# A fused linear attention and smoothed-ReLU MLP kernel: third group loaded whole, one table less, last output block in halves, a new order of the steps

## The chip, the cores and the metric

The kernel runs on one core of a Trainium2 chip. Its engines are TensorE (PE, with its weight loads listed apart as PEld), VectorE (DVE), ScalarE (ACT), GpSimd (POOL) and SyncE (SP), which issues most of the transfers. The metric is the time of one execution on the device in microseconds.

## The reference

Four sequences of 768 steps, 8 heads of 48 channels, go through a decayed linear attention; its output, seen as 3072 tokens of 384 channels, goes through an MLP with 2048 hidden channels.

```python
for t in range(S):                                   # r, k, v: (4, 8, 768, 48)
    cur = einsum('bhd,bhe->bhde', u * k[t], v[t])
    y[t] = einsum('bhd,bhde->bhe', r[t], state + cur)
    state = w[:, None] * state + einsum('bhd,bhe->bhde', k[t], v[t])
h = y.reshape(3072, 384) @ w_in                      # 384 x 2048
g = where(h >= 1, h, where(h <= -1, 0, (h + 1) ** 2 / 4))
out = g @ w_out                                      # 2048 x 384
```

## The kernel before

**Tiling.** Time is cut into 6 chunks of 128 steps. A unit is one sequence in one chunk; two units make a group, so there are 12 groups (0 to 11) and 24 units (0 to 23). Unit n is half n % 2 of group n // 2. Groups 0 and 1 are the first chunk. Within a chunk the recurrence becomes matrix products: A is K times R transposed, masked to AT; Y is AT times V plus R times the carried state; Sp is what the chunk adds to the state.

**The order.** The kernel is one list of words, ORDER, written out by hand (lines 24 to 59). The loop at its end (line 529) calls one function for each word, in that order, and every engine runs its own instructions strictly in the order in which they were issued. A word has the step's name, the group or unit, after a dot the half (or, for m, r, s, g, the quarter of the hidden channels, and for M first the half and then the quarter), after = the engine (V is DVE, A is ACT, G is POOL) and after / the PSUM banks. So the order of the words with one engine is that engine's queue, and a step waits behind all words of its engine that stand ahead of it.

**The steps.**
- LR, LK, LV: loads of r, k, v (line 252, on SP's queue); without a half, both halves in one transfer.
- ln, bw, bu, wq, wE, wC, uS, WupS, WdnS, Wup, Wdn: tables of powers of w and of u. Wup and Wdn write a second copy of a table to PSUM, which the scaled R and K of group 0 then read.
- Rs, Ks: R and K scaled by their tables. KU, RKU, us, B: the term of u.
- TR, TK, T: transposes on PE, copied out by cR, cK, c; from group 4 on RT and KT do it by a transposing transfer. A (and AA for both units), AT (mask, on DVE), V (cast of v, on ACT), Y, y and yg, X with its copy xc, from group 3 on xcg in place of both (a transposing transfer).
- Sp, Tm, decayg, sbf: the state.
- m: a quarter of the first projection, 12 matmuls of 256 columns into a pair of PSUM banks; r, s, g: its activation, on ACT, ACT and DVE. The pair is free when g is done.
- M: an eighth of the second projection, 4 matmuls of 384 columns; og or o copies the result out, stg or st stores it. WI and WO load w_in and w_out on POOL's queue, in 3 and 2 parts.
- Zs and Z: n matmuls on a tile of zeros, to keep PE running.

**PSUM.** Two pairs of banks (0 and 1) exist all the time. Four single banks serve groups 0 and 1; when the first step asks for pair 2 or 3, they are closed and become those two pairs (line 185).

**Around the change.** Group 2 is loaded in six halves (LR2.0 to LV2.1). Rs of group 0 reads the PSUM table of Wup. Group 11 has no group behind it: its two halves have a PSUM pair each and use only the first bank of the two, so each is copied (o11.0 on ACT, o11.1 on DVE) and stored on its own.

Of the kernel before, what the change touches and what calls it, by code (L numbers as in the profile page):

```python
# [73 lines left out]
def kernel(  # L74
# [35 lines left out]
    def copy(e, out, in_):  # L110
        nc.scalar.copy(out, in_) if e == "A" else engines[e].tensor_copy(out, in_)  # L111
# [379 lines left out]
    def do_M(e, b, g, jq):  # L491
        j, q = jq
        last = g == S // C * BP - 1
        key, k = (("op", g, j), 0) if last else (("op", g), j)
        if key not in tiles:
            tiles[key] = pair(b[0], F32, "op")
        wi, wo = part(q, OUT_PARTS)
        for f in range(FG):
            nc.tensor.matmul(  # L499
                tiles[key][:, k, :DO], tiles["g", g, q][:, f, j * P : (j + 1) * P], w_out_sb[wi][:, wo, f * DO : (f + 1) * DO],  # L500
                start=(q == 0 and f == 0), stop=(q == nQ - 1 and f == FG - 1),
            )
# [21 lines left out]
    def do_Z(e, b, n):  # L524
        for i in range(n):
            nc.tensor.matmul(tiles["z"][:, 0, :P], idle[:, :P], idle[:, :P], start=True, stop=True)

# [39 lines left out]
```

## Time and profile before

| | us |
|---|---|
| median of 3 runs | 174.38 |
| lowest and highest of them | 174.08, 174.93 |
| the profiled execution | 173.8 |
| span of its trace | 172.0 |
| PE busy in the span | 163.7 |
| DVE, ACT, POOL busy | 130.6, 130.0, 117.1 |

The span runs from the first instruction to the last; some 1.8 us of the execution lie around it. PE is busy for 95% of the span, the others for 68 to 76%. The granted TensorE clock is 1.00 in all of it. In rows of the trace a time is followed by the duration; a row with x60 stands for 60 instructions, and what stands in brackets is the idle time just before it and what ended it.

### The profile page before, as it was taken

How to read it: one execution, taken by the hardware profiler on the slowest of the kernel's cores; microseconds unless marked ns; L12 is line 12 of the kernel's file. 1: busy time of each engine (PE TensorE's matmuls, PEld its weight loads, DVE VectorE, ACT ScalarE, POOL GpSimd, SP SyncE). 2: the span in 40 equal slices, each digit the busy share in tenths (PEclk: the TensorE clock that was granted, in tenths of full speed). 3: DMA queues.
4: the chain of work that ended last, by engine and by line, in shares of the span. 5: the costliest groups of instructions: out<-in, count | busy, mean ns of one | idle time of the engine just before them, and what ended most of it. 6: DMA issues, size and time to landing. Idle time of an engine off the chain costs nothing.

```text
span 172.0 us, 4014 instructions
## 1 busy us (share of the span) xinstructions
PE 163.7 (95%) x1658; PEld 130.9 (76%) x1658; DVE 130.6 (76%) x149; ACT 130.0 (76%) x150; POOL 117.1 (68%) x85
## 2 busy tenths in 40 slices
...
GB/s 106 198 187 191 199 203 197 221 195 203 174 190 88 213 188 175 188 204 150 200 312 197 185 215 174 219 173 168 308 195 219 4 60 138 43 98 0 8 91 91
DMA packets 103591, 28.26 MB, mean 164 GB/s; under 512 B 98834, under 2 KB 102676, under 8 KB 103572
## 3 DMA queue, kind: packets, MB, share of 16 engines
...
q0 software_dynamic: 1744, 3.15, 10.0%
q8 instruction: 13, 0.21, 0.5%
...
q10 hardware_dynamic: 4, 0.00, 0.0%
...
## 4 chain that ended last, share of the span: by engine, by line
PE 81%; DMA 5%; SPq 4%; ACT 3%; POOL 2%; DVE 2%; issue 1%; DVEq 0%; POOLq 0%
PE hp L464 36%; PE op L499 34%; SPq L252 4%; PE A L359 3%; DMA Vi<-in_v_dram 3%; DMA xT<-y 2%; PE Y L427 2%; PE Y L421 2%; PE Sp L394 2%; ACT pt L475 1%; ACT Vb L111 1%; POOL V L302 1%; PE T L319 1%; DVE g L487 1%; POOL RKU L271 1%
## 5 line engine op out<-in xcount | busy, mean ns | idle before, releaser
L464 PE MATMUL hp<-xT,w_in 128*128 128x256 bf16 x576 | 69.1, 273 | 0.9 <-DMA xT<-y 0.5
L499 PE MATMUL op<-w_out,g 128*128 128x384 bf16 x384 | 68.4, 326 | 0.0
L487 DVE SCALAR_TENSOR_TENSOR g<-sq,hp 128x1024 bf16<-128x1024 bf16 x48 | 57.9, 1215 | 13.2 <-ACT sq L484 13.2
L464 PEld LDWEIGHTS <-w_in 128*128 128x128 bf16 x576 | 61.9, 114 | 4.2 <-issue 1.2
L475 ACT ACTIVATE pt<-hp 128x1024 f32<-128x1024 f32 x46 | 46.9, 1020 | 14.0 <-PE hp L464 14.0
L499 PEld LDWEIGHTS <-g 128*128 128x128 bf16 x384 | 36.3, 98 | 21.3
L484 ACT ACTIVATE sq<-pt 128x1024 bf16<-128x1024 f32 x46 | 48.3, 1057 | 1.2
L368 DVE TENSOR_TENSOR AT<-A,umask 128x1024 bf16<-128x1024 f32 x20 | 23.7, 1219 | 5.2 <-PE A L359 5.2
L271 POOL TENSOR_TENSOR Ks<-Ki,Wdn 128x768 bf16<-128x768 f32 (+1 forms) x12 | 20.2, 1684 | 7.4 <-DMA Ki<-in_k_dram 3.7
L302 POOL TENSOR_TENSOR V<-Vb,diag 128x768 f32<-128x768 bf16 (+1 forms) x14 | 18.1, 1292 | 10.2 <-DVE diag L293 4.4
L271 POOL TENSOR_TENSOR RKU<-Ri,KU 128x768 f32<-128x768 f32 (+1 forms) x13 | 21.2, 1631 | 1.2 <-DVE KU L271 0.8
L405 POOL TENSOR_TENSOR state<-Tm,wCm 128x768 f32<-128x768 f32 x8 | 14.6, 1822 | 10.6 <-DVE Tm L402 10.6
L271 POOL TENSOR_TENSOR KU<-Ki,u_sb 128x768 f32<-128x768 f32 (+1 forms) x13 | 21.2, 1632 | 0.4 <-DMA Ki<-in_k_dram 0.3
L271 POOL TENSOR_TENSOR Rs<-Ri,Wup 128x768 bf16<-128x768 f32 x10 | 18.2, 1824 | 0.0
L439 DVE TENSOR_TENSOR y<-Y,V 128x768 bf16<-128x768 f32 x10 | 9.6, 956 | 5.9 <-PE Y L427 3.3
L111 ACT CAST Vb<-Vi 128x768 bf16<-128x768 f32 (+1 forms) x14 | 10.2, 734 | 4.8 <-DMA Vi<-in_v_dram 4.8
L293 DVE TENSOR_REDUCE diag<-RKU 128x16 f32<-128x768 f32 (+1 forms) x14 | 11.6, 830 | 1.5 <-POOL RKU L271 1.5
L111 ACT COPY o<-op 128x768 f32<-128x768 f32 (+1 forms) x9 | 6.9, 764 | 6.4 <-PE op L499 6.3
L111 ACT CAST state_bf<-state 128x768 bf16<-128x768 f32 (+1 forms) x12 | 8.5, 717 | 3.7 <-POOL state L405 3.7
L427 PE MATMUL Y<-Vb,AT 128*128 128x48 bf16 x192 | 10.2, 185 | 0.4 <-ACT Vb L111 0.4
L427 PEld LDWEIGHTS <-AT 128*128 128x128 bf16 x192 | 9.3, 97 | 0.7 <-issue 0.5
L402 DVE TENSOR_TENSOR Tm<-Sp,state 128x768 f32<-128x768 f32 x8 | 7.6, 956 | 2.7 <-PE Sp L394 2.7
...
## 6 DMA issues: line engine op xcount, KB each, us to landing
out_dram<-o SPq DMA_DIRECT2D x11, 384.0 KB, 3.9
Ki<-in_k_dram SPq DMA_DIRECT2D x9, 384.0 KB, 6.0
Ri<-in_r_dram SPq DMA_DIRECT2D x9, 384.0 KB, 6.1
Vi<-in_v_dram SPq DMA_DIRECT2D x9, 384.0 KB, 5.0
...
Ki<-in_k_dram SPq DMA_DIRECT2D x6, 192.0 KB, 3.9
Ri<-in_r_dram SPq DMA_DIRECT2D x6, 192.0 KB, 4.6
Vi<-in_v_dram SPq DMA_DIRECT2D x6, 192.0 KB, 5.4
```

What stands on the lines that cost most here:

```text
L111: nc.scalar.copy(out, in_) if e == "A" else engines[e].tensor_copy(out, in_)
L271: engines[e].tensor_mul(part(out)[:, :, :, :D], part(a), rep(b, j1 - j0) if len(b.shape) == 3 and b.shape[1] == H else part(b))
L293: nc.vector.tensor_reduce(d[:, hs], tiles["RKU", g][:, hs, :], AX.X, ALU.add)
L302: engines[e].tensor_mul(t[:, hs, :], tiles["V", g][:, hs, :], tiles["diag", g][:, hs].unsqueeze(2).to_broadcast([P, n, D]))
L368: nc.vector.tensor_mul(t.rearrange("p i n t -> p (i n) t"), tiles["A", n].rearrange("p i (n t) -> p (i n) t", t=P), umask.unsqueeze(1).to_ ...
L405: engines[e].tensor_mul(states[g % BP], tiles["Tm", g], flat(wCm).unsqueeze(1).to_broadcast([P, UNITS, DM]))
L427: nc.tensor.matmul(Y[:, h * D : (h + 1) * D], AT[:, i, p, :], V[:, j * H + h, :], start=(c == 0), stop=True, skip_group_check=True,)
L464: nc.tensor.matmul(hp[:, f, :], w_in_sb[wi][:, i, wo * FG * P + f : (wo + 1) * FG * P : FG], tiles["xT", g][:, :, i, :], start=(i == 0), s ...
L475: nc.scalar.activation(t, tiles["hp", g, q], AF.Relu, bias=0.5, scale=0.5)
L484: nc.scalar.activation(t, p, AF.Square)
L487: nc.vector.scalar_tensor_tensor(out=make("g", ("g", g, q), [P, FG, TOK], BF16), in0=tiles["sq", g, q], scalar=1.0, in1=tiles["hp", g, q], ...
L499: nc.tensor.matmul(tiles[key][:, k, :DO], tiles["g", g, q][:, f, j * P : (j + 1) * P], w_out_sb[wi][:, wo, f * DO : (f + 1) * DO], start=( ...
```

## The change

The list ORDER is replaced as a whole; the number of instructions of each kind stays, but for what follows.
- LR2, LK2, LV2 load group 2 in three transfers, where six were.
- The word Wup is gone, so Rs of group 0 reads the table in SBUF.
- Group 11 writes its second projection with 8 matmuls of 192 columns for each M, the two halves of the output columns in the two banks of the pair. M11.13 becomes MA11.13 and MB11.13, one for each half of the columns, and o11.1 and st11.1 become oA11.1, stA11.1, oB11.1, stB11.1.
- Some steps change engine. To DVE come KU0.1, Ks1.0, KU1.0, RKU1.0, cR0, cR1, cK2, cK3, wC, xc1, KU3, og0, c6, xc4, r2.2, og3 and og9; from DVE go uS, cR3, r1.2, c4, xc5, og4, og10 (to ACT), Rs1.0, Rs1.1 and RKU0.1 (to POOL); s0.2 goes from ACT to POOL.
- The PSUM banks of many steps change. The Z's are 19, 3, 10, 12, 9, 5 and 2 matmuls, 60 as before.
- The tile of zeros has 128 columns instead of 512. New functions gate, do_HR, do_HK and do_Zq are called by no word.

```diff
-Zs/0 ln Z19 bw/1 LK0.0 bu/0 uS=V LK1.0 LR0.0 LK0.1 LR0.1 LV0.0 wq/2 WdnS Ks1.0=G LR1.0 LR1.1 Wdn/3 Ks0.0=V Ks0.1=V
-TK0/0 Wup/1 Rs0.0=V TR0/3 LK1.1 cK0=A WupS KU0.1=G KU0.0=V RKU0.0=G cR0=A KU1.0=G LV0.1 Rs0.1=V Z2 TR1/1 A0/03 LV1.0
-LV1.1 WI0 WI1 WI2 us0.0 cR1=A TK1/1 cK1=A AT0.1 Z4 A1/13 Rs1.0=V LR2.0 LR2.1 Rs1.1=V V0.1 AT1.0 V0.0 Z9 TR3/1 B0.0=G
-AT1.1 RKU0.1=V wE AT0.0 wC=A us0.1 Z7 Y1/3 TR2/0 B0.1=G Y0/2 y0 y1 cR2=A RKU1.0=G Z8 X0/2 Z4 TK2/3 X1/0 Ks1.1=G xc0=A
-Sp1/2 cK2=A xc1=A Z7 TK3/3 cK3=A Tm1 A2/20 m0.0/0 cR3=V us1.0 AT2.1 AT2.0 r0.0=A A3/31 AT3.1 KU1.1=G RKU1.1=G m0.1/1
-V1.0 s0.0=A B1.0=G Sp2/2 AT3.0 us1.1 r0.1=A Tm2 Y2/3 y2 g0.0 V1.1 X2/0 LK2.0 Y3/1 B1.1=G s0.1=A LK2.1 Sp0/2 Sp3/3
-xc2=V LK3 y3 WO0 m0.3/0 r0.3=A s0.3=A g0.1 X3/1 Tm0 xc3=V m0.2/1 LR3 LV2.0 Tm3 m1.1/2 g0.3 r1.1=V m1.0/3 m1.2/0 Ks2=G
-r0.2=A s0.2=A g0.2 sbf2=A s1.1=A r1.0=A s1.0=A sbf3=A g1.1 m1.3/1 r1.2=V WO1 KU2=G LV2.1 M0.00/2 M0.10 M0.11 M0.01
-g1.0 M1.00/3 M1.10 M1.11 M1.01 Rs2=G s1.2=A g1.2 T5/0 RKU2=G LK4 r1.3=A s1.3=A g1.3 T4/1 LV3 Ks3=G M0.02 M0.03 LR4 us2
-c5=V A5/0 KU3=G Rs3=G c4=V A4/1 AT5 sbf1=A M1.02 M0.12 M0.13 AT4 T6/0 sbf0=A V2 Y4/1 Y5 B2=G og0=A T7/2 c6=A RKU3=G
...
-r3.2 s3.2=A KT5 m3.3/1 M3.00/3 M3.10 V5 B4=G AT8 Y8/2 Y9 r3.3 g3.2 s3.3=A LK8 M3.11 M3.12 M3.01 M3.02 yg4 AA5/20 g3.3
-M3.13 M3.03 xcg4 m4.0/1 LR7 KU5=G RKU5=G AT10 LK7 decayg3=G sbfg3=A Rs6=G og3=A us5 LV7 B5=G KU6=G RKU6=G r4.0 Sp8/2
...
-yg11 xcg11 m10.3/0 M10.00/3 g10.1 M10.10 r10.3 m10.2/1 s10.3=A g10.3 r10.2 M10.11 M10.01 s10.2=A m11.0/2 g10.2 r11.0
-m11.1/0 M10.02 M10.03 r11.1 s11.0=A m11.2/1 g11.0 M10.12 M10.13 s11.1=A r11.2 g11.1 m11.3/2 og10=V s11.2=A M11.10/0
-M11.11 g11.2 stg10 r11.3 s11.3=A M11.00/3 M11.01 M11.12 M11.02 g11.3 M11.13 M11.03 o11.1=V st11.1 o11.0=A st11.0
+Zs/0 LR0.0 LK0.0 LR0.1 LV0.0 LR1.0 ln Z19 bw/3 LK1.0 bu/1 WupS Rs0.0=V Rs0.1=V Wdn/0 LK0.1 WdnS uS=A KU0.0=V LV0.1
+TR0/2 RKU0.0=G wq/3 Ks0.0=V Rs1.0=G TK0/1 LR1.1 cR0=V wE wC=V LK1.1 WI0 us0.0 V0.0 TR1/2 KU0.1=V RKU0.1=G cK0=A Z3
+A0/31 Ks0.1=V Z10 TK1/0 cK1=A cR1=V LV1.0 AT0.0 LV1.1 WI1 V0.1 AT0.1 us0.1 Z12 A1/31 AT1.1 Sp0/2 Y0/0 B0.0=G AT1.0
+Rs1.1=G Z9 TR3/1 B0.1=G y0 Ks1.0=V Y1/3 y1 LR2 KU1.0=V WI2 cR3=A Z5 X0/1 xc0=A Z2 X1/0 xc1=V RKU1.0=V TR2/1 cR2=A Tm0
+TK2/3 cK2=V Ks1.1=G KU1.1=G m0.0/1 A2/10 us1.0 TK3/2 cK3=V AT2.0 AT2.1 m0.1/0 r0.0=A A3/23 s0.0=A r0.1=A AT3.0 Sp1/1
+Tm1 g0.0 RKU1.1=G V1.0 B1.0=G Sp2/0 Y2/2 AT3.1 m0.2/1 WO0 s0.1=A LK2 g0.1 us1.1 V1.1 B1.1=G Y3/1 LR3 y2 m0.3/0 r0.2=A
+Tm2 y3 r0.3=A s0.3=A X2/3 xc2=V Sp3/0 s0.2=G Tm3 X3/2 xc3=V m1.2/2 m1.0/3 LK3 g0.3 m1.1/0 Rs2=G WO1 r1.2=A s1.2=A g0.2
+g1.2 m1.3/1 r1.0=A KU2=G s1.0=A r1.1=V Ks2=G g1.0 s1.1=A r1.3=A M0.00/2 M0.01 M0.10 M0.11 g1.1 M1.00/3 sbf0=A RKU2=G
+T5/0 c5=V s1.3=A sbf2=A Rs3=G M1.01 LV2 g1.3 LV3 M1.10 T4/0 M0.12 c4=A LR4 A5/1 Ks3=G sbf3=A us2 M1.11 AT5 V2 A4/0 AT4
+M1.12 KU3=V M0.02 M0.03 LR5 B2=G T6/0 c6=V M0.13 T7/1 og0=V Y4/0 sbf1=A Y5 c7=A LK4 RKU3=G M1.02 A6/2 yg2 M1.03 V3 AT6
+X5/1 X4/0 xc4=V xc5=A LK5 M1.13 Rs4=G us3 og1=A A7/1 m2.0/2 r2.0=A B3=G Y6/0 s2.0=A Sp4/3 RT4 AT7 Y7 yg3 m2.1/1 r2.1=A
...
+M2.03 LV6 M2.12 M2.13 sbfg2=A Ks5=G KU5=G og2=A g3.0 us4 V4 AA4/21 LV5 m3.2/0 m3.3/3 AT8 AT9 Y8/2 r3.2 B4=G decayg3=G
+KT5 Y9 yg4 xcg4 RKU5=G s3.2=A LR9 LK7 M3.00/1 M3.10 M3.01 M3.11 g3.2 M3.12 M3.02 r3.3 KU6=G s3.3=A g3.3 M3.03 LK9 us5
+sbfg3=A V5 B5=G AA5/23 AT10 m4.0/0 r4.0 M3.13 Ks6=G KT6 AT11 s4.0=A m4.1/2 og3=V r4.1 Y10/3 Y11 RKU6=G s4.1=A stg0
...
+AA11/02 AT22 M9.03 AT23 s10.0=A sbfg9=A M9.12 M9.13 m10.1/0 Y22/2 Y23 g10.0 m10.2/1 r10.1 s10.1=A yg11 xcg11 r10.2
+M10.00/2 M10.10 og9=V m10.3/3 stg9 s10.2=A g10.1 M10.01 g10.2 m11.1/0 M10.11 M10.12 m11.0/1 r10.3 s10.3=A g10.3 r11.1
+s11.1=A M10.02 r11.0 s11.0=A m11.2/3 g11.1 g11.0 m11.3/0 M10.03 r11.2 s11.2=A M10.13 g11.2 M11.10/1 M11.11 r11.3
+s11.3=A g11.3 M11.00/3 M11.01 M11.02 M11.03 og10=A stg10 o11.0=A st11.0 M11.12 MA11.13 oA11.1=A stA11.1 MB11.13
+oB11.1=A stB11.1
-    idle = const.tile([P, 512], BF16, name="idle")
+    idle = const.tile([P, P], BF16, name="idle")
...
-    def do_M(e, b, g, jq):
+    def do_M(e, b, g, jq, halves=(0, 1)):
...
-        key, k = (("op", g, j), 0) if last else (("op", g), j)
+        key = ("op", g, j) if last else ("op", g)
...
-        for f in range(FG):
-            nc.tensor.matmul(
-                tiles[key][:, k, :DO], tiles["g", g, q][:, f, j * P : (j + 1) * P], w_out_sb[wi][:, wo, f * DO : (f + 1) * DO],
...
+        for i, o0, o1 in [(i, i * DO // 2, (i + 1) * DO // 2) for i in halves] if last else [(j, 0, DO)]:
+            for f in range(FG):
+                nc.tensor.matmul(
+                    tiles[key][:, i, : o1 - o0], tiles["g", g, q][:, f, j * P : (j + 1) * P], w_out_sb[wi][:, wo, f * DO + o0 : f * DO + o1],
...
+    def do_MA(e, b, g, jq):
+        do_M(e, b, g, jq, (0,))
+    def do_MB(e, b, g, jq):
+        do_M(e, b, g, jq, (1,))
...
+    def half_out(e, g, j, i):
+        cols = slice(i * DO // 2, (i + 1) * DO // 2)
+        copy(e, make("o", ("o", g, j), [P, UNITS, DO], F32)[:, 0, cols], tiles["op", g, j][:, i, : DO // 2])
...
+    def half_st(g, j, i):
+        cols = slice(i * DO // 2, (i + 1) * DO // 2)
+        nc.sync.dma_start(out=rows_out(g, j, j + 1)[:, :, cols], in_=tiles["o", g, j][:, 0:1, cols])
...
-        copy(e, make("o", ("o", g, j), [P, UNITS, DO], F32)[:, 0], tiles["op", g, j][:, 0, :DO])
+        o = make("o", ("o", g, j), [P, UNITS, DO], F32)[:, 0]
+        copy(e, o.rearrange("p (i d) -> p i d", i=2), tiles["op", g, j][:, :, : DO // 2])
```

More of the change, by code (lines that the diff above doesn't have):

```diff
@@ L252, in load, with gate, do_HR, do_HK @@
         nc.sync.dma_start(out=t[:, j0 * H : j1 * H, :], in_=source(x, g, j0, j1))
+    def gate(e, what, cls, g):
+        engines[e].memset(make(cls, (what, g), [P, UNITS * H, D], F32)[:1, :1, :1], 0.0)
+    def do_HR(e, b, g):
+        gate(e, "R", "Ri", g)
+    def do_HK(e, b, g):
+        gate(e, "K", "Ki", g)
     def do_LR(e, b, g, j=None):
@@ L497, in do_M @@
         wi, wo = part(q, OUT_PARTS)
-        for f in range(FG):
-            nc.tensor.matmul(
-                tiles[key][:, k, :DO], tiles["g", g, q][:, f, j * P : (j + 1) * P], w_out_sb[wi][:, wo, f * DO : (f + 1) * DO],
-                start=(q == 0 and f == 0), stop=(q == nQ - 1 and f == FG - 1),
-            )
+        for i, o0, o1 in [(i, i * DO // 2, (i + 1) * DO // 2) for i in halves] if last else [(j, 0, DO)]:
+            for f in range(FG):
+                nc.tensor.matmul(
+                    tiles[key][:, i, : o1 - o0], tiles["g", g, q][:, f, j * P : (j + 1) * P], w_out_sb[wi][:, wo, f * DO + o0 : f * DO + o1],
+                    start=(q == 0 and f == 0), stop=(q == nQ - 1 and f == FG - 1),
+                )
+    def do_MA(e, b, g, jq):
+        do_M(e, b, g, jq, (0,))
+    def do_MB(e, b, g, jq):
+        do_M(e, b, g, jq, (1,))
     def rows_out(g, j0, j1):
```

46 lines of the change are left out of this document (27 added, 19 removed).

## The prediction

> **What bounds the kernel now.** First the table of stages, then the chain that ended last.
>
> ```profile
> 20.00:30.00 10.00, 8.15 (x98) 7.44 (x97) 8.75 (x15) 8.20 (x10) 4.93 (x6) 1.00 1.12 201
> 30.00:40.00 10.00, 10.00 (x85) 7.71 (x84) 9.21 (x9) 8.40 (x11) 9.98 (x7) 1.00 1.04 202
> ...
> 60.00:80.00 20.00, 19.53 (x221) 15.84 (x220) 16.11 (x16) 15.64 (x17) 17.89 (x12) 1.00 1.12 181
> ...
> 160.00:172.00 12.00, 8.51 (x59) 5.65 (x56) 6.12 (x6) 5.58 (x7) 0.00 (x0) 1.00 0.19 68
> ```
>
> The columns after the length are busy time of PE, PEld, DVE, ACT and POOL, granted clock, DMA share, GB/s. In the rows from 30 on, the five left out being full, PE misses 0.47 us between 60 and 80 and what follows its last matmul. The chain says the same and gives the dates:
>
> ```profile
> 8.61 4.67 DMA Vi<-in_v_dram
> ...
> 27.09 6.73 PE hp L464 x60
> 33.82 5.20 PE op L499 x32
> ...
> 57.58 1.31 PE hp L464 x12
> ...
> 68.47 0.06 PE Y L427 x2
> 68.63 0.96 DVE y L439
> 69.61 3.90 DMA xT<-y
> 73.56 1.47 PE hp L464 x12
> ...
> 163.31 5.21 PE op L499 x32
> 168.54 0.48 ACT o L111
> ```
>
> So the time has three parts. **Front:** until 33.82, when M0.00 starts; the projections of groups 0 and 1 and all work of units 0 to 3 are done by then, in both orders. **Middle:** 33.82 to 168.5, on PE alone, with one hole, at m4.0. **Tail:** 168.5 to 172.0. The multiplications behind M0.00 are the same in both, so the middle can change only by holes. What counts is the date of M0.00, the holes, and the tail.
>
> **The front.** Rows for it, from the timeline:
>
> ```profile
> 4.85 1.48 PE L210 MATMUL up<-u_row,ones 1*128 1x384 f32 x2
> ...
> 10.75 2.47 POOL L243 DMA_DIRECT2D w_in<-in_moe_w_in_dram  x3
> 11.30 1.01 DVE L271 TENSOR_TENSOR Rs<-Ri,Wup 128x384 bf16<-128x384 f32 x2
> 12.58 1.14 PE L526 MATMUL z<-idle 128*128 128x128 bf16 x9
> 12.69 1.29 DVE L373 TENSOR_TENSOR AT<-A,umask 128x512 bf16<-128x512 f32 x2 [0.37 <-PE A L359]
> 15.52 0.61 PE L526 MATMUL z<-idle 128*128 128x128 bf16 x8
> 18.36 0.41 DVE L111 COPY TT<-TR 128x512 bf16<-128x512 bf16 x1
> 19.04 1.50 PE L464 MATMUL hp<-xT,w_in 128*128 128x256 bf16 x12
> 20.57 1.03 ACT L475 ACTIVATE pt<-hp 128x1024 f32<-128x1024 f32 x1 [1.18 <-PE hp L464]
> 22.04 1.05 ACT L484 ACTIVATE sq<-pt 128x1024 bf16<-128x1024 f32 x1
> 23.55 1.21 DVE L487 SCALAR_TENSOR_TENSOR g<-sq,hp 128x1024 bf16<-128x1024 bf16 x1
> 27.42 0.35 DVE L111 COPY xT<-X 128x384 bf16<-128x384 bf16 x1
> ```
>
> Loads first. LV0.1 is the tenth half load and landed at 8.61 + 4.67 = 13.28. A half is 0.197 MB, and
>
> ```profile
> q1 hardware_dynamic: 976, 0.18, 141.1%
> ```
>
> is what the queue of the loads moved from 8 to 9 us: 0.19 MB (976 packets of 192 bytes), so a half takes 1.03 us. By that the k-th half lands at 2.98 + 1.03 k. In the new order LV0.1 is the eighth (11.2), LR1.0 the fifth (8.1), LR1.1 the ninth (12.3), but LK0.1 the seventh (10.2) where it was the fourth (7.1). So DVE, which has KU0.1 and Ks0.1 now, cannot pass 10.2 before that load. Dropping Wup/1 takes one table (about 0.5 us) off ACT while it waits for loads anyway: nothing. Rs of group 0 from SBUF costs DVE 0.505 a half, as the row for Wup shows: nothing.
>
> From 10.2 DVE has, in order: KU0.1 Ks0.1 cR1 AT0.0 AT0.1 us0.1 AT1.1 AT1.0 y0 Ks1.0 y1 KU1.0 xc1 RKU1.0 Tm0 cK2 us1.0 cK3 AT2.0 AT2.1 AT3.0 Tm1 g0.0 AT3.1 g0.1 us1.1 y2 Tm2 y3 xc2 Tm3 xc3. Sixteen of these are half products, sums or additions at 0.51 (1.01 for two), 8.2 us; eight AT at 0.645 (1.29 for two), 5.2; three copies of TT at 0.38, 1.1; three of xT at 0.31, 0.9; two g at 1.18, 2.4. That is 17.8 us.
>
> How far m0.0 gets by it: the first twelve up to KU1.0 are 6.5 us (7 x 0.51, 4 x 0.645, one 0.38), so KU1.0 ends about 17.0 with 0.2 of waiting, xc1 at 17.3, and after TR2 and TK2 m0.0 starts at about 17.7, 1.3 us before the 19.04 of the trace. But the gain does not last. m0.2 waits for g0.0, m0.3 for g0.1, and all of y2, y3, xc2, xc3 follow them on DVE. g0.0 has AT3.0 and Tm1 ahead of it and ends at 23.5 (24.8 in the trace); xc3 ends at 10.2 + 17.8 + waits. Waits I count: A1 needs the banks that AT0.1 frees (0.1), cK3 needs m0.0 and A2 ahead of TK3 on PE (0.3). So xc3 is at 28.4, less 0.1 because the two waits overlap others: 28.3. Then m1.2 starts (its pair of banks and its xT both wait for the last xc and Tm3), and m1.2, m1.0, m1.1, m1.3 at 1.31 bring M0.00 to 33.6. Before: 33.82. **The front gives 0.2**, though the first projection comes 1.3 earlier: DVE got 2 us more to do (KU0.1, Ks1.0, KU1.0, RKU1.0, cR0, cR1, cK2, cK3, xc1, wC come; uS, Rs1.0, Rs1.1, RKU0.1, cR3 go) and takes the rest back. Bounds: all 1.3 if DVE is never behind, and -1.0 if each of the ten changes of engine below costs 0.1 of waiting.
>
> Two clocks of z stand above: 9 in 1.14, 8 in 0.61, with the granted clock at 1.00 in both; in this trace PE doubles its rate between 14 and 15.5. In the new order PE is busy nearly without a break from 8.4 (TK0, TR1, Z3, A0, Z10, TK1, Z12). The Trainium skill, page "TensorE: Matmul & The Clock Gate", section "Part 1: The HAM clock gate", says that PE starts at half rate and is released after about 4 us of sustained activity. By it Z12 would run fast and A1 start 0.1 earlier, 173.3 in place of the forecast below; by the trace's own date it stays slow until 14 and A1 is where I put it.
>
> **Weights.** WI0 stood on POOL at 10.75 with WI1 and WI2 behind it. Now POOL runs RKU0.0, Rs1.0, WI0, RKU0.1, WI1, B0.0, Rs1.1, B0.1, WI2. POOL's prices:
>
> ```profile
> L271 POOL TENSOR_TENSOR Rs<-Ri,Wup 128x768 bf16<-128x768 f32 x10 | 18.2, 1824 | 0.0
> ...
> L271 POOL TENSOR_TENSOR RKU<-Ri,KU 128x384 f32<-128x384 f32 x3 | 3.0, 1002 | 0.9 <-DVE KU L271 0.8
> ```
>
> The matmul for u ends at 6.33 as before, uS on ACT takes 0.48, KU0.0 on DVE 0.55, so RKU0.0 runs from 7.65 and Rs1.0 to 9.65: WI0 at 9.65, 1.1 earlier. RKU0.1 waits for KU0.1 (10.7): WI1 at 11.8, 0.2 later. B0.0, Rs1.1, B0.1 (0.8, 1.0, 0.8) bring WI2 to 15.2, 2.8 later. What such a weight does to loads:
>
> ```profile
> q0 software_dynamic: 142, 0.15, 92.8%
> q1 hardware_dynamic: 228, 0.04, 32.8%
> ```
>
> In the stretch 13 to 14 weights (q0) got 0.15 MB/us and loads 0.04. From 12 to 13 it had been
>
> ```profile
> q0 software_dynamic: 1, 0.00, 1.8%
> ```
>
> one packet, so the first bytes come about 2 behind the issue. WI0 and WI1 together are 0.79 MB and WI2 the same: q0 is busy from 11.6 to about 22. m0.2 needs WI2 at 23.5, so 1.5 is left. The loads LK1.1, LV1.0, LV1.1 crawl meanwhile and land by my sum at 16.5, 19 to 21, 23; Ks1.1, V1.0 and V1.1 are due at 16, 22.2 and 23.7. I cost this at nothing: m0.1 on PE covers Ks1.1, r0.1 and s0.1 on ACT cover the V's. LR2, LK2, LV2 whole instead of by halves move the same bytes behind all of these, and their first users (T5 at 37) are 10 us away: nothing. The Trainium skill, page "DMA: Bandwidth & Descriptors", section "Queues, rings and completion order", has each DMA engine take turns between its queues packet by packet. Taken as one packet each, 142 loads of 192 bytes a microsecond, 0.027 MB, would pass; V1.0 would then come 0.9 late and the time be 174.3. The trace's 228 against 142 is more than that.
>
> s0.2 goes from ACT to POOL, a size that POOL has no row for. Between 384 and 768 elements it pays 2.15 ns each; by that 1024 cost 2.4 (bounds 1.8 and 3.6, one and two products of 768). It lies behind B1.1, which ends about 26.7 (us1.1 at 25.8); Rs2, WO1, KU2, Ks2 wait for it. WO1 goes out at 31, and M0.12 needs it at 39 (5 M, T5, 2 M, T4 after 33.6). Two us to the first byte and 0.79 MB at 0.15 bring it to 38: covered by 1 us, no more. T5 needs Ks2, at 35.3 with 37 the need: covered.
>
> **The middle.** The hole:
>
> ```profile
> 73.56 1.47 PE L464 MATMUL hp<-xT,w_in 128*128 128x256 bf16 x12 [0.47 <-DMA xT<-y]
> ```
>
> Y9 ended at 68.53 and m4.0 could start at 73.56, 5.0 later; between them stood six M (0.65 each, 5.20/8) and AA5 (0.55), 4.45. Now seven M and AA5 stand there: 5.1. The hole closes: **0.47 gained** (bounds 0 and 0.47). What would be late next is m11.1, with 4.57 behind Y23; there xT has no loads to meet, and the median landing is
>
> ```profile
> xT<-y SPq DMA_TRANSPOSE x9, 3.0
> ```
>
> 0.96 + 3.0 + 0.1 = 4.1: no hole. Elsewhere the new order keeps distances like those that ran without a hole (first M behind its projection 3.7 in both).
>
> **The tail.**
>
> ```profile
> GB/s 0 0 0 0 0 0 0 0 0 0 0 0 0 261 307 384 353 384 231 338 307 430 323 430 169 16 0 0 0 0 0 0 0 0 0 0 0 0 0 0
> ...
> out_dram<-o SPq DMA_DIRECT2D x2, 192.0 KB, 1.9
> ```
>
> ```profile
> 169.05 0.34 SPq L515 DMA_DIRECT2D out_dram<-o  x1
> ```
>
> ```profile
> L111 ACT COPY o<-op 128x768 f32<-128x768 f32 x8 | 6.4, 800 | 3.4 <-PE op L499 3.2
> ...
> L111 ACT COPY o<-op 128x384 f32<-128x384 f32 x1 | 0.5, 478 | 3.1 <-PE op L499 3.1
> ```
>
> Today: last matmul T = 168.50, copy 0.48, issue at T + 0.55, the stores' bytes (slices of 0.1 us from 168) at 0.39 MB in 1.2 us, so 0.6 for one. New: MA11.13 ends at T - 0.33; a copy of 192 columns is 0.32 by the two rows; stA is issued at T + 0.06 and keeps SP until T + 0.4; oB ends at T + 0.36, stB goes at T + 0.43, 0.12 earlier. Half the bytes: 0.3 less (bounds 0, if landing has one price, and 0.3). Against it, 32 M become 64 of half the width: a matmul of 384 columns takes 162.5 ns, of 256 109.2, so 2.5 ns each are fixed: 0.08. og10 on ACT lies before M11.03 ends. **The tail gives 0.34** (0.04 to 0.4).
>
> **The sum.** 0.2 + 0.47 + 0.34 = 1.0. The profiled execution took 173.8 (span 172.0): 172.8. It lies 0.6 under the median of 174.38; off that median the forecast is 173.4.
>
> **The rivals.** *DVE is never behind.* The front keeps m0.0's 1.3: 174.38 - 1.3 - 0.8 = 172.3. For it: DVE is busy 8.75 of 10 us in 20 to 30, not all. Against: g0.0 and g0.1 stand behind three AT. *DVE or a new hole takes it all* (waits at each changed engine, c6 behind KU3 on DVE with 0.2 to spare before Y4, WO1): 1.0 lost, 174.4. *WI2 comes late*, on the slow side. Of the weights before, WI0 had
>
> ```profile
> w_in<-in_moe_w_in_dram POOLq DMA_DIRECT2D x1, 384.0 KB, 5.5
> ```
>
> 5.5 to landing: 2 to the first byte and 3.5 for 0.39 MB, 0.11 MB/us against loads. If loads hold all three weights to that, WI2 lands at 11.6 + 1.57/0.11 = 25.9, 2.4 behind the need of m0.2, with V1.1 behind it: 175.8. It decides from a landing after 23.5, and each us later is a us of the time. For it: four loads are still in the queue when WI0 starts. Against: from 13 to 14 the weight already had 0.15. *The change does nothing where it says*: whole loads are the same bytes; that is inside the first case.
>
> **How the numbers follow.** Forecast 173.4: 0.42, own range 172.9 to 173.9. Never behind, 172.3: 0.19. All taken, 174.4: 0.16. WI2 late, 175.8: 0.23. About 0.5% is what a measurement of this kernel can tell from no change: 173.5 and 175.25. The forecast's case gives 0.27 to faster, 0.15 to same; with 172.3 faster is 0.46; 174.4 and the near end of the late weight make same 0.33; slower 0.21. The range 172.1 to 175.5 leaves out a little of 172.3 and somewhat over half of the late weight, 2 in 10.
>
> **What would show it.** m0.0 near 17.7; xc3 near 28.3 with DVE full from 10.2; M0.00 near 33.6; PE whole between 60 and 80; 3.1 to 3.2 us from the last matmul to the end where there were 3.5. Wrong if PE waits for w_in before m0.1 or m0.2, for w_out before M0.12, or for xT elsewhere; or if DVE idles before 28 while M0.00 comes late.

## The result, and the profile after

| | before | after |
|---|---|---|
| median of 20 executions each, us | 174.37 | 176.17 |
| lowest, highest | 173.81, 175.25 | 174.82, 177.22 |
| ratio of the times, 95% interval | | 1.0082 [1.0061, 1.0104] |
| profiled execution, span | 173.8, 172.0 | 175.03, 173.3 |

The change makes the kernel 0.8% slower, where 0.6% faster was forecast. The 20 executions of after fall into two groups of ten: those with a granted clock of 0.997 to 1.000 have a median of 175.10, those with 0.99 one of 176.78. So there are two losses: 0.73 us (0.4%) by which the first group lies above the median before, and 1.7 us more in the second. The profiled execution is of the first group. The ratios here and below leave out executions more than 1.5% above the fastest of their kernel; the counts by clock keep them, but for one of e14 that took 279.06.

The table of stages of after, with the columns as before:

```profile
20.00:30.00 10.00, 7.38 (x97) 6.49 (x92) 8.85 (x17) 7.49 (x9) 4.69 (x5) 1.00 1.05 194
...
60.00:80.00 20.00, 20.00 (x219) 16.01 (x218) 17.01 (x18) 15.73 (x18) 17.66 (x11) 1.00 1.15 185
80.00:100.00 20.00, 19.68 (x198) 14.91 (x196) 16.11 (x15) 16.66 (x18) 17.41 (x11) 1.00 1.11 221
...
160.00:173.30 13.30, 9.62 (x98) 8.67 (x96) 4.12 (x4) 7.48 (x10) 0.00 (x0) 1.00 0.18 61
```

PE is busy for 0.77 us less between 20 and 30 (7.38 for 8.15), it is whole between 60 and 80 as forecast, and it misses 0.32 between 80 and 100, where it missed nothing before. The chain of after gives the dates:

```profile
29.30 5.40 PE hp L475 x48
34.70 3.25 PE op L512 x20
...
94.59 2.91 DMA KT<-Ks
...
162.88 6.26 PE op L512 x68
```

M0.00 starts at 34.70, 0.88 later than before; all dates of M0.00 below are those of the chain, which starts a step when the one ahead of it has ended (in the timeline its first row starts some 0.16 earlier). From there to the end of the last matmul (170.04) it is 135.34 us, where it was 134.68 (168.50 less 33.82). The tail is 3.26 (173.3 less 170.04), where it was 3.50. So 0.88 + 0.66 - 0.24 = 1.30, the difference of the spans. That is more than the 0.73 between the medians, since the profiled execution of before lies 0.57 under its median, that of after 0.07 under the median of its group.

### The profile page after: what moved, and what is told of

It is laid out like the page before. It is cut to its first block, busy times and chain, and to the rows that moved or that the text cites. A ratio compares the mean times of both kernels' runs of the same rounds, so it can differ in the third digit from the quotient of the medians.

```text
span 173.3 us, 4072 instructions
## 1 busy us (share of the span) xinstructions
PE 163.8 (95%) x1690; PEld 132.1 (76%) x1690; DVE 135.3 (78%) x156; ACT 126.0 (73%) x144; POOL 116.7 (67%) x84
## 3 DMA queue, kind: packets, MB, share of 16 engines
q0 software_dynamic: 1744, 3.15, 10.2%
## 4 chain that ended last, share of the span: by engine, by line
PE 82%; DVE 8%; ACT 2%; issue 2%; DMA 2%; SPq 1%; POOL 0%; ACTq 0%; POOLq 0%
PE op L512 35%; PE hp L475 31%; PE A L370 4%; DVE AT L384 2%; PE Y L438 2%; DVE g L498 2%; PE Y L432 2%; DMA KT<-Ks 2%; PE z L566 1%; PE Sp L405 1%; PE T L330 1%; PE wp L233 1%; PE lwp L207 1%; DVE y L446 1%; DVE state L409 1%
## 5 line engine op out<-in xcount | busy, mean ns | idle before, releaser
L512 PE MATMUL op<-w_out,g 128*128 128x384 bf16 (+1 forms) x416 | 68.6, 314 | 0.4 <-ACT o L112 0.4
L512 PEld LDWEIGHTS <-g 128*128 128x128 bf16 x416 | 38.5, 98 | 20.0 <-issue 0.6
L495 ACT ACTIVATE sq<-pt 128x1024 bf16<-128x1024 f32 x45 | 47.5, 1058 | 1.3
L379 DVE TENSOR_TENSOR AT<-A,umask 128x1024 bf16<-128x1024 f32 x20 | 23.6, 1219 | 4.7 <-PE A L370 4.6
L282 POOL TENSOR_TENSOR Ks<-Ki,Wdn 128x768 bf16<-128x768 f32 (+1 forms) x11 | 19.3, 1756 | 3.9 <-PE Sp L405 2.4
L282 POOL TENSOR_TENSOR Rs<-Ri,Wup 128x768 bf16<-128x768 f32 (+1 forms) x12 | 20.3, 1690 | 0.6 <-DMA Ri<-in_r_dram 0.6
L282 POOL TENSOR_TENSOR KU<-Ki,u_sb 128x768 f32<-128x768 f32 (+1 forms) x10 | 17.8, 1780 | 0.0
L304 DVE TENSOR_REDUCE diag<-RKU 128x16 f32<-128x768 f32 (+1 forms) x14 | 11.6, 830 | 0.0
L112 ACT COPY o<-op 128x768 f32<-128x768 f32 (+2 forms) x10 | 6.7, 673 | 5.7 <-PE op L512 5.7
L112 ACT CAST Vb<-Vi 128x768 bf16<-128x768 f32 (+1 forms) x14 | 10.2, 734 | 0.0
L438 PE MATMUL Y<-Vb,AT 128*128 128x48 bf16 x192 | 10.2, 183 | 0.0
```

What stands on the lines that cost most here:

```text
L282: engines[e].tensor_mul(part(out)[:, :, :, :D], part(a), rep(b, j1 - j0) if len(b.shape) == 3 and b.shape[1] == H else part(b))
L304: nc.vector.tensor_reduce(d[:, hs], tiles["RKU", g][:, hs, :], AX.X, ALU.add)
L379: nc.vector.tensor_mul(t.rearrange("p i n t -> p (i n) t"), tiles["A", n].rearrange("p i (n t) -> p (i n) t", t=P), umask.unsqueeze(1).to_ ...
L438: nc.tensor.matmul(Y[:, h * D : (h + 1) * D], AT[:, i, p, :], V[:, j * H + h, :], start=(c == 0), stop=True, skip_group_check=True,)
L495: nc.scalar.activation(t, p, AF.Square)
L512: nc.tensor.matmul(tiles[key][:, i, : o1 - o0], tiles["g", g, q][:, f, j * P : (j + 1) * P], w_out_sb[wi][:, wo, f * DO + o0 : f * DO + o1 ...
```

## The experiments

The theories: **D**, three products that went to DVE are slow there; **W**, the third part of w_in lands late; **F**, the order of the words around m0.2 keeps back work that could fill the wait; **H**, the clock falls because PE has little work from 22 to 25 us; and for the rest, that a wait on a copy eats the tail's gain, and that SP's queue keeps KT7 back. Ratios are to the kernel before, on the same chip.

### The slow products and the late weight: e1_psum, e2_wi2, e3_both

The timeline of after, DVE (KU0.1, then the three products) and then POOL, around m0.0:

```profile
10.49 0.55 DVE L282 TENSOR_TENSOR KU<-Ki,u_sb 128x384 f32<-128x384 f32 x1
...
15.26 0.94 DVE L282 TENSOR_TENSOR Ks<-Ki,Wdn 128x384 bf16<-128x384 f32 x1
16.59 1.08 DVE L282 TENSOR_TENSOR KU<-Ki,u_sb 128x384 f32<-128x384 f32 x1
17.87 1.08 DVE L282 TENSOR_TENSOR RKU<-Ri,KU 128x384 f32<-128x384 f32 x1
```

```profile
17.20 1.34 POOL L282 TENSOR_TENSOR KU<-Ki,u_sb 128x384 f32<-128x384 f32 x1
18.61 1.20 POOL L282 TENSOR_TENSOR RKU<-Ri,KU 128x384 f32<-128x384 f32 x1
```

The prediction had 0.51 for each of the three; they take 0.94, 1.08 and 1.08 while POOL works beside them, and POOL's own two take 1.34 and 1.20 where 1.00 was its price. KU0.1, the same product as the second of the three, took 0.55 while POOL had nothing to do (from 10.47 to 11.13). And the third weight is late on PE:

```profile
24.73 1.50 PE L475 MATMUL hp<-xT,w_in 128*128 128x256 bf16 x12 [0.84 <-DMA w_in<-in_moe_w_in_dram]
```

e1_psum puts the table of Ks and of u into PSUM for the three, so that each has one operand there. e2_wi2 moves WI2 ahead on POOL. e3_both does both.

```diff
 e1: -... bu/1 ... Wdn/0 LK0.1 WdnS uS=A KU0.0=V
     +... bu/1 ... Wdn LK0.1 WdnS uS=A uT KU0.0=V
     (Wdn and a copy of u in the two banks of pair 1; Ks1.0, KU1.0, RKU1.0 read them)
 e2: -LV1.1 WI1 V0.1 ... KU1.0=V WI2 cR3=A
     +LV1.1 WI1 WI2 V0.1 ... KU1.0=V cR3=A
```

> The changed kernel, but with copies of the tables Wdn and u in pair 1 of PSUM, read by the three DVE products of unit 2 (Ks1.0, KU1.0, RKU1.0), so that each reads only one operand from SBUF; same order, same engines. Theory A (in the changed kernel these three took 0.94, 1.08 and 1.08 us because they read two operands from SBUF beside a POOL product): each takes 0.55 to 0.6, POOL's KU1.1 and RKU1.1 1.0 instead of 1.34 and 1.20; M0.00 starts 0.4 to 0.9 us before the 34.70 of the changed kernel. Rival B (the late w_in part alone holds the front): durations may fall, m0.2 still starts at 24.7 and M0.00 at 34.6 to 34.7. Rival C (DVE's products are slow for another reason, such as their place in the order): the durations stay near 1 us.

> The changed kernel with WI2 directly behind WI1 on POOL, ahead of B0.0, Rs1.1 and B0.1; nothing else. Theory A (DVE is the bound of the front): the wait of 0.84 us on w_in before m0.2 goes, but m0.2 then waits for g0.0 and starts at 24.5 instead of 24.73; M0.00 0.0 to 0.3 us earlier than 34.70. Rival B (the late weight is the bound): M0.00 0.8 us earlier, at 33.9.

> Both edits of the two runs before together. If DVE and the weight hold the front in turn, M0.00 starts at 33.5 to 34.0, earlier than with either alone, and the span falls by 0.7 to 1.2 us from 173.3. If only one of them counts, it is as with that one.

Measured: 1.0075 [1.0041, 1.0110], 1.0111 [1.0087, 1.0136] and 1.0058 [1.0029, 1.0088]; M0.00 at 34.78, 35.91 and 34.53. In e1 the three products are back at 0.54 to 0.55, but DVE waits instead. Its rows in e1, and those of m0.0 and m0.1 on PE:

```profile
17.20 0.54 DVE L307 TENSOR_TENSOR RKU<-Ri,tabs 128x384 f32<-128x384 f32 x1
...
19.97 0.43 DVE L112 COPY TT<-TK 128x512 bf16<-128x512 bf16 x1 [0.96 <-PE TK L343]
...
22.15 0.69 DVE L397 TENSOR_TENSOR AT<-A,umask 128x512 bf16<-128x512 f32 x1 [0.56 <-PE A L383]
```

```profile
17.80 1.47 PE L488 MATMUL hp<-xT,w_in 128*128 128x256 bf16 x12 [0.46 <-DVE RKU L307]
...
20.28 1.50 PE L488 MATMUL hp<-xT,w_in 128*128 128x256 bf16 x12 [0.35 <-DMA w_in<-in_moe_w_in_dram]
```

What the three products won, some 1.5 us, DVE idles away at cK3 (0.96, TK3 stands behind m0.0 on PE) and AT3.0 (0.56, A3 stands behind m0.1). A part of this the edit itself brings: m0.0 uses the pair of banks in which the tables lie and waits 0.46 until RKU1.0 has read them. m0.1 then waits 0.35 for the second part of w_in. So D's mechanism is shown, and so is that taking its price away does not by itself bring M0.00 forward. The Trainium skill, page "SBUF — State Buffer", section "SBUF: two separate sides", says that VectorE and GpSimd share one pair of ports under an exclusive lock, which an operation of VectorE with two SBUF inputs needs against an operation of GpSimd that reads SBUF. The rows agree: 1.08 with both inputs in SBUF beside POOL, 0.55 with one in PSUM, 0.55 with both in SBUF and POOL idle.

W alone is not borne out either. With WI2 issued ahead of B0.0, Rs1.1 and B0.1, e2 has no wait for it: it landed at 23.6, 10.7 behind its issue. But the first product was still slower there (Ks1.0 took 1.92), and M0.00 came later still, so e2 does not price the weight alone. In e3, without the slow products, m0.2 waits 0.68 and starts at 24.40, and M0.00 gains 0.17. In before, after, e1 and e3 the weight landed between 24.3 and 25.0.

### The order around m0.2: e11_reorder, e12_reorder_alone

The chain of after in the front runs on DVE alone from 20.6 to 29.3, but for one product on POOL. Its end:

```profile
24.41 0.68 DVE AT L384
25.09 1.13 DVE g L498
26.22 0.48 DVE diag L304
...
26.84 0.83 POOL V L313
...
27.70 0.56 DVE y L446
28.25 0.27 DVE xT L112
...
28.98 0.28 DVE xT L112
```

The sum us1.1 (diag) stands behind g0.1 although its input was there at 19.8, and B1.1, y3, xc3 and m1.2 wait for it. In before, us1.1 ran at 22.14:

```profile
22.14 0.54 DVE L293 TENSOR_REDUCE diag<-RKU 128x8 f32<-128x384 f32 x1
```

On PE, m0.2, which waits for w_in, stands ahead of Y3, X2, Sp3 and X3. e11_reorder is e1 with V1.0, V1.1, us1.1, B1.1 and RKU1.1 moved ahead of r0.0, g0.0 ahead of AT3.0 and Tm1, and Y3, Sp3 and X2 ahead of m0.2; e12_reorder_alone has the same words without e1's tables.

```diff
-... us1.0 TK3/2 cK3=V AT2.0 AT2.1 m0.1/0 r0.0=A ... g0.0 RKU1.1=G V1.0 B1.0=G Sp2/0 Y2/2 AT3.1 m0.2/1 ... g0.1 us1.1 V1.1 B1.1=G Y3/1
+RKU1.1=G ... us1.0 V1.0 V1.1 B1.0=G TK3/2 us1.1 B1.1=G cK3=V AT2.0 AT2.1 m0.1/0 r0.0=A ... Y2/2 AT3.1 Y3/1 Sp3/3 y2 ... y3 X2/2 m0.2/1 g0.1
```

> The changed kernel with the tables of the three early products of group 1 in PSUM (as in the first experiment, where this alone left M0.00 at 34.78), and the words between m0.0 and m1.2 in another order: V1.0, V1.1, us1.1 and RKU1.1 ahead of r0.0, and Y3, Sp3 and X2 ahead of m0.2. Theory F: the third weight slice still lands at 24.3 to 25.0 and m0.2 starts there, but no transposition is left behind it but X3, so m1.2 starts at 27.9 to 28.4 (29.38) and M0.00 at 33.3 to 33.9; span 172 to 172.6. Theory D (only the slow products matter) and theory W (only the landing of the weights matters): M0.00 34.5 to 34.9 as without the order.

> The same order of the words, with the tables in SBUF as the changed kernel has them. Theory F with D beside it: the products of group 1 take 0.9 to 1.1 us again and VectorE comes about 1 us later to m0.0, of which some half is left at m1.2: m1.2 at 28.3 to 29.0, M0.00 at 33.7 to 34.4, between the two. Theory D alone: 34.6 to 34.9. Theory H: the stretch without TensorE work at 22 to 25 us is still there in this and the last kernel, so that the clock of 0.99 may be seen in some executions of both.

PE in e11, from m0.2 on:

```profile
24.86 1.47 PE L488 MATMUL hp<-xT,w_in 128*128 128x256 bf16 x12
26.17 0.33 PE L473 MATMUL X<-ident,y 128*128 128x128 bf16 x3
26.41 4.28 PE L488 MATMUL hp<-xT,w_in 128*128 128x256 bf16 x36
31.35 2.78 PE L488 MATMUL hp<-xT,w_in 128*128 128x256 bf16 x24 [0.66 <-DVE g L511]
33.96 0.49 PE L525 MATMUL op<-w_out,g 128*128 128x384 bf16 x2
```

m1.2 now follows m0.3 without a break (at some 27.8, a third into the row of 36), where it came at 29.30 in after and 29.38 in e1. A new wait of 0.66 for a g stands later, and M0.00 is at 34.13 in the chain, 0.65 earlier than in e1 and 0.57 earlier than in after, though not at the 33.3 to 33.9 expected. So F is right for M0.00 where the tables are in PSUM; which of the moved words does it was not separated. But the span is 173.9 and the ratio 1.0086 [1.0056, 1.0116]: the end did not move. The profiled execution of e12 (1.0104 [1.0065, 1.0143]) had a clock of 0.987 and M0.00 at 36.37. It can be set only beside e13 below, whose clock fell to half in the same stretch (24.8 to 28.2 and 24.9 to 28.3) and which has M0.00 at 35.99. In this one pair the order alone brings M0.00 no gain, so that the 0.65 seems to need both edits.

### The clock: e13_again, e5_fill

e13_again is the changed kernel, unaltered; its profile caught an execution at 0.99. e5_fill has 10 matmuls on zeros ahead of Sp2 and 14 behind Y2, in free columns of those banks.

```diff
-B1.0=G Sp2/0 Y2/2 AT3.1
+B1.0=G Sb2/0 ZS2 Sp2/0 Y2/2 ZY2 AT3.1
```

> The changed kernel again, unaltered, for one more profile. About half of its executions have a granted clock of 0.99 and are 1.7 us longer; should this be one, theory H says that the rows of its clock by windows show one drop of some 3.4 us at half rate, beginning between 22 and 27 us, and full rate everywhere else. If it is an execution at full clock it says nothing.

> The changed kernel with 10 matmuls on zeros ahead of Sp2 and 14 behind Y2, into the free columns of their PSUM banks, where PE waited (22.5 to 23.4 and 23.9 to 24.7 us); nothing else. In 10 of 20 executions of the changed kernel the granted clock averages 0.99 and the time is 1.7 us longer; in none of 49 of the kernel before. Theory H (the sparse stretch of PE between 22 and 25 us lets the clock gate close for one window of about 3.4 us at half rate): with the filling the executions at 0.99 become rare, at most 1 in 8; the others stay at 174.8 to 175.5, the ratio falls from 1.008 to 1.004. Rival (the clock dips elsewhere, as in the long dense stretch): the share stays near one half.

The table of stages of e13, the granted clock is the third column from the end:

```profile
24.50:25.00 0.50, 0.40 (x3) 0.36 (x4) 0.50 (x1) 0.16 (x1) 0.41 (x1) 0.89 0.37 75
25.00:26.00 1.00, 1.00 (x7) 0.74 (x5) 1.00 (x2) 0.00 (x0) 0.00 (x0) 0.50 0.70 123
26.00:27.00 1.00, 1.00 (x7) 0.69 (x6) 1.00 (x3) 0.00 (x0) 0.16 (x1) 0.50 1.08 141
27.00:28.00 1.00, 1.00 (x13) 0.82 (x12) 0.92 (x3) 0.82 (x1) 0.66 (x1) 0.50 0.88 160
28.00:29.00 1.00, 1.00 (x10) 0.88 (x9) 0.25 (x1) 0.21 (x1) 0.72 (x1) 0.85 1.08 206
```

The clock is at half rate from about 24.9 to 28.3: 0.11 us in the first row (a mean of 0.89 over 0.5 us), 3 us, and 0.30 in the row of 28 (0.85 over 1 us), together 3.41 us, which cost 1.7. m0.2 falls into it and takes 2.54 instead of 1.50. The 3.4 us ahead of it, in the tables of before, e13, e5 and after (the first number behind the length is PE's busy time):

```profile
21.50:24.90 3.40, 2.00 (x37) 1.71 (x35) 3.40 (x7) 3.38 (x6) 1.25 (x2) 1.00 1.15 212
```

```profile
21.50:24.90 3.40, 1.78 (x31) 1.27 (x29) 3.38 (x6) 2.91 (x5) 1.52 (x2) 1.00 1.02 195
```

```profile
21.50:24.90 3.40, 2.83 (x52) 2.23 (x49) 3.38 (x6) 2.91 (x5) 1.51 (x2) 1.00 1.07 206
```

```profile
21.50:24.90 3.40, 1.65 (x30) 1.14 (x28) 3.38 (x6) 2.91 (x5) 1.51 (x2) 1.00 1.05 199
```

PE was busy for 2.00 of them in before, 1.78 in e13 and 2.83 in e5, and for 1.65 in the profiled execution of after, whose clock did not fall. So the sparse stretch is what makes the drop possible, and does not bring it every time. With the words of after in this stretch, 33 of 85 executions (after, e1 to e4, e6, e13, e14) had a clock of 0.99 or less, with the words of e11 and e12, sparser still (1.51 in e11), 10 of 18, with those of before (before, e7 to e10) 4 of 158, and with e5's filling none of 12. e5 itself is at 1.0052 [1.0032, 1.0072]: the filling takes away the drop and not the other loss. Its profiled execution, at full clock, has a span of 174.8 and waits of 0.39, 0.27 and 0.34 for transposing transfers behind M0.00, where after has one of 0.32. So H holds: the drop follows the sparse stretch and goes when it is filled. The Trainium skill, page "TensorE: Matmul & The Clock Gate", section "Part 1: The HAM clock gate", has the gate judge by a free-running window of 3.4 us; the length of the drop and its coming in some executions only agree. The page's row for half rate names an idle window; here one that was 52% busy (1.78 of 3.40) was enough.

### The tail: e4_tail_undone, e6_tail_free, e7_before_tail

The end of after:

```profile
169.17 0.32 ACT L112 COPY o<-op 128x192 f32<-128x192 f32 x1 [0.51 <-PE op L512]
...
169.54 0.49 PE L512 MATMUL op<-w_out,g 128*128 128x192 bf16 x4 [0.41 <-ACT o L112]
```

MB11.13 waits 0.41 for ACT's copy oA11.1: both belong to one PSUM tile, and the write of one half waits for the read of the other. e4 takes the last M whole with one copy and one store; e6 gives the second half of the columns a PSUM pair of its own; e7 is the kernel before with its tail in halves in two pairs.

```diff
 e4: -M11.12 MA11.13 oA11.1=A stA11.1 MB11.13 oB11.1=A stB11.1
     +M11.12 M11.13 o11.1=A st11.1
 e6: -M11.10/1 M11.11 ... M11.02 M11.03 og10=A stg10 o11.0=A st11.0 M11.12 MA11.13 oA11.1=A stA11.1 MB11.13
     +MA11.10/1 MA11.11 ... M11.02 MA11.12 M11.03 og10=A stg10 MA11.13 o11.0=A st11.0 oA11.1=A stA11.1 MB11.10/2 MB11.11 MB11.12 MB11.13
 e7: -M11.00/3 M11.01 M11.12 M11.02 g11.3 M11.13 M11.03 o11.1=V st11.1 o11.0=A st11.0
     +MA11.00/3 MA11.01 M11.12 MB11.00/1 MB11.01 MA11.02 g11.3 M11.13 o11.1=V st11.1 MA11.03 oA11.0=A stA11.0 MB11.02 MB11.03 oB11.0=A stB11.0
```

> The changed kernel with M11.13 whole, one copy o11.1 on ACT of 384 columns and one store. Theory T (in the changed kernel MB11.13 waits 0.41 us for the copy oA11.1, because both touch one PSUM tile, and the halves give back there what they save): no such wait, the last matmul ends 0.5 to 0.6 us earlier, the stretch from it to the end is 3.5 us as in the kernel before instead of 3.26; span 0.3 to 0.4 us shorter than 173.3. Rival (the halves do save): span 0.2 to 0.3 us longer.

> The changed kernel with the second half of the columns of unit 23 in a PSUM pair of its own (pair 2), its four M of 192 columns behind all others, so that they wait for no copy. Theory T (the halves save 0.3 to 0.5 us once MB does not wait for oA): no wait of PE on ACT in the last 10 us, the last matmul ends near 169.4 to 169.5 instead of 170.04, the stretch behind it is 3.1 to 3.3 us, span 172.6 to 172.9. Rival (two stores at the end cost what the shorter copy saves): the stretch behind it grows to 3.5 and the span stays at 173.2.

> The order of the kernel before, with only the tail in halves, and in a pair of its own as in the run before (unit 22 last, its second half in pair 1). By theory T: 0.3 to 0.5 us faster than the kernel before, ratio 0.997 to 0.998; no execution at a clock of 0.99, as its front is that of the kernel before. Rival: ratio 1.000.

Measured: 1.0063 [1.0031, 1.0095], 1.0033 [1.0001, 1.0066] and 1.0014 [0.9995, 1.0033]. In e4 the wait is gone and the last matmul ends at 169.67, but the tail is 3.73: its span, 173.4, is that of after (173.3). So the halves win some 0.47 behind the last matmul (3.73 less 3.26) and lose about as much ahead of it. In e6 the wait on ACT is gone, a wait for g11.2 (0.23) stands in its place, and the last matmul ends at 170.03 as in after. Yet the eight executions of e6 at full clock have a median of 175.10, and before has 175.09 on this chip; the profile shows no gain to match, and whether the tail in its own pair makes that difference stays open. e7 shows no gain in the kernel before either.

### Whole loads and one table less: e8_before_parts

The kernel before with LR2, LK2 and LV2 whole and without Wup.

```diff
-TK0/0 Wup/1 Rs0.0=V ... LR2.0 LR2.1 ... LK2.0 Y3/1 B1.1=G s0.1=A LK2.1 ... LV2.0 Tm3 ... LV2.1
+TK0/0 WupS Rs0.0=V ... LR2 ... LK2 Y3/1 B1.1=G s0.1=A ... LV2 Tm3
```

> The kernel before with two parts of the change alone: LR2, LK2 and LV2 whole, and the word Wup gone (WupS in its place), Rs of group 0 from SBUF; order and tail otherwise as before. My prediction: nothing, ratio 0.998 to 1.002. Rival (whole loads of group 2 come in the way of the weights or the values): slower by 0.3% or more, with a wait on w_in or on V before m0.2.

1.0006 [0.9983, 1.0029]: nothing, as the prediction costed them.

### What the middle gives back: e9_front, e14_kt7, e10_best

e9_front has the words of before up to M0.00 and those of after from there on. e14_kt7 is after with KT7 and stg2 exchanged on SP's queue. e10_best is e9 with that exchange and e4's tail.

```diff
 e14: -g5.1 stg2 yg6 Sp11 xcg6 ... M5.01 KT7 M5.11
      +g5.1 KT7 yg6 Sp11 xcg6 ... M5.01 stg2 M5.11
```

> The changed kernel with the words of the kernel before up to M0.00 (its own words from there on, tail in halves included). Theory F (the loss lies in the order of the front: in TensorE's order m0.2 waits for the third weight slice ahead of Y3, X2, Sp3 and X3) and theory H (the sparse stretch of TensorE at 22 to 25 us is what lets the clock drop to 0.99 in half of the executions): M0.00 at 33.6 to 34.0 instead of 34.70, the rest as in the changed kernel (135.3 us to the last matmul, 3.2 of tail), span 172.2 to 172.8, and a granted clock of 0.99 in at most 1 of 12 executions; ratio to the kernel before 0.999 to 1.004. Rival (the loss or the drops of the clock lie behind M0.00): span 173 or more, or 3 and more of 12 executions at 0.99.

> The changed kernel with two words of SyncE exchanged: KT7 stands where stg2 stood and stg2 where KT7 stood. Theory Q (SyncE's queue, issue behind issue from 53 to 98 us, sets when KT7 goes out, and TensorE only meets it at AA7): KT7 issued at about 90 instead of 94.59, RT7 at about 92.7, no hole at AA7 (0.32), the last matmul 0.3 earlier (169.6 to 169.8), span about 173.0, ratio to the kernel before 0.2% lower than the changed kernel's, with the same drops of the clock. Rival (the DMA engines are full and only the bytes count): the hole moves to another step of the same size, and the last matmul stays at 170.0.

> The front of the kernel before (as in e9_front, where M0.00 came at 33.84 and the span stayed 173.7), KT7 ahead of stg2 as in the run before this one, and the last unit whole with one store (as in e4_tail_undone). Theory Q: the 0.86 us of the front and the holes at AA7 and behind oA11.1 all reach the end, last matmul at 168.2 to 168.9, tail 3.7, span 171.9 to 172.6, a clock of 0.99 in at most 1 of 12, ratio 0.993 to 1.000. Rival (the bytes): another transfer is late, a hole of 0.5 to 1 us stands elsewhere between 60 and 100 us, span 173 or more, ratio 1.001 to 1.004.

e9 has M0.00 at 33.89 and one execution of 12 under 0.99, both as expected, but a span of 173.7, for 172.2 to 172.8 expected, and 1.0035 [1.0010, 1.0060]. SP's queue in e9, and then in after:

```profile
90.12 1.68 SPq L525 DMA_DIRECT2D out_dram<-o  x1
91.89 1.24 SPq L434 DMA_TRANSPOSE xT<-y  x1
93.25 1.37 SPq L285 DMA_TRANSPOSE RT<-Rs  x1
94.67 1.30 SPq L285 DMA_TRANSPOSE KT<-Ks  x1
```

```profile
89.96 1.79 SPq L558 DMA_DIRECT2D out_dram<-o  x1
91.85 1.26 SPq L467 DMA_TRANSPOSE xT<-y  x1
93.22 1.32 SPq L318 DMA_TRANSPOSE RT<-Rs  x1
94.59 1.30 SPq L318 DMA_TRANSPOSE KT<-Ks  x1
```

Issue stands behind issue with 0.05 to 0.12 between them, and KT7 goes out at the same time in both (94.67 and 94.59), though PE is 0.81 ahead at M0.00. So PE waits longer at AA7, 0.64 instead of 0.32, and starts it at 97.79 instead of 97.55: by then the gain of the front has been given back. In e14, SP's queue and the waits of PE:

```profile
90.78 2.46 SPq L318 DMA_TRANSPOSE KT<-Ks  x1
93.33 1.23 SPq L467 DMA_TRANSPOSE xT<-y  x1
```

```profile
96.19 1.50 PE L475 MATMUL hp<-xT,w_in 128*128 128x256 bf16 x12 [0.26 <-DMA xT<-y]
110.73 0.62 PE L370 MATMUL A<-RT,KT 48*128 48x128 bf16 x16 [0.82 <-DMA KT<-Ks]
```

KT7 is early and AA7 does not wait, but the issue takes 2.46 instead of 1.30, the transposing transfer behind it goes out 1.5 later (93.33 for 91.85), and the holes are 0.26 and 0.82: 1.0093 [1.0053, 1.0133], no better than after. The rival, that the hole moves, was right, and the holes are larger than the one they replace. In e10 M0.00 itself waits 0.35 for w_out (34.15). Behind it no wait reaches 0.2, no execution of 12 is under 0.99, and the ratio is 0.9993 [0.9971, 1.0015]: equal to the kernel before, and no version beat before. Its last matmul ends at 169.47, where 168.2 to 168.9 was expected; what holds it was not found. The ratio is 0.4% under that of e9, on another chip; which of the two edits made it was not separated, nor whether the time of the issues themselves or the transfers ahead of them set that row.

## Why the prediction was wrong

In the profiled executions the front came out at -0.88, where +0.2 was forecast, and what follows M0.00 at -0.42 (138.60 for 138.18), where middle and tail were to give 0.81.

**The step that failed** is "The front gives 0.2", and in it the sum "Sixteen of these are half products, sums or additions at 0.51" with its 0.3 of waiting. Three of the sixteen took 0.94, 1.08 and 1.08, 1.57 more than 3 x 0.51. The mechanism of the step was right: DVE was full from 10.2 and set m1.2, but xc3 ended at 29.25 instead of 28.3, m0.0 started at 18.00 instead of 17.7 and M0.00 at 34.70 instead of 33.6. The 1.57 is not the whole of it: KU0.1 started at 10.49 instead of 10.2, and the rest of the list took 0.9 less than summed, so that the two errors partly cancel (0.29 + 1.57 - 0.91 = 0.95). The prediction took the duration of a product from rows with POOL at other work. That removing this price brought nothing in e1, where cK3 and AT3.0 wait 1.52, and that the order then brought 0.65 in e11, shows a second omission: the list of DVE was summed in order, with 0.3 of waiting, and not asked whether us1.1 and B1.1 behind g0.1, or Y3 behind m0.2, could be late.

**Weights.** By "q0 is busy from 11.6 to about 22" WI2 had 1.5 to spare at 23.5; it landed at about 24.7. The issues came as forecast (9.54, 12.07, 15.41 for 9.65, 11.8 and 15.2). The rival "WI2 comes late" was right that it would, but not that "each us later is a us of the time": m0.2 waited 0.84 and is not on the chain in after.

**The clock.** PE's rows in after where the prediction weighed the rule of the Trainium skill:

```profile
0.99 2.21 PE L566 MATMUL z<-idle 128*128 128x128 bf16 x19 [0.99 <-DVE idle L134]
...
9.93 0.61 PE L370 MATMUL A<-TT 48*128 48x128 bf16 x8
...
11.96 1.26 PE L566 MATMUL z<-idle 128*128 128x128 bf16 x12
13.15 0.40 PE L370 MATMUL A<-TT 48*128 48x128 bf16 x8
```

A1 takes 0.40 where A0, ahead of it, took 0.61, so PE runs at the higher rate from about 13.15, earlier than the 14 to 15.5 read from the trace of before. By the rule, about 4 us of activity, this fits only if the count starts near 8.64, as the prediction started it (8.4). The profile has PE busy from 0.99 on, with one gap of 0.20 ahead of 3.40, and from there it took some 12 us; so this trace does not bear the rule out, and why the earlier work did not count is open. The tenth it was worth is not seen at M0.00. What the same gate cost behind the sparse stretch, 1.7 us in half of the executions, no case of the prediction had. With full clock throughout the median would be 175.1 (estimated from the ten executions at full clock), inside the range but still slower than before.

**s0.2 on POOL** took 1.88, for which 2.4 was taken with bounds of 1.8 and 3.6; nothing waited for it. The whole loads and the missing table cost nothing (e8). WO1 and T5 made no hole.

**The middle** closed the hole at m4.0, as forecast, but 0.32 of the 0.47 was given back at AA7: "Elsewhere the new order keeps distances like those that ran without a hole" was wrong there. The hole at m4.0 is not one size, either: in before it is 0.47 in the profiled execution, and with the same words 1.36 in e7 and 1.16 in e8.

**The tail.** 3.26 behind the last matmul, just above the 3.1 to 3.2 forecast. What was not seen is that MB11.13 waits for oA11.1, ahead of the last matmul: 0.41, and 0.17 more, since its four matmuls take 0.50 of the chain behind the wait and 0.33 without one (6.59 for 72 in e4 less 6.26 for 68). The split of the M's cost some 0.08 as forecast. The net is nothing (e4).
